# Output weights of a cached decode step: rows of 4 KB for four heads in place of 2 KB for two

## The chip, the cores and the metric

The kernel runs on one core of a Trainium2 chip. The metric is the device time of one launch in microseconds (us), as a median of several runs; runs of most kernels agree within about 0.3 us, apart from a few that are 1 to 2 us longer. A run of one core alone has its state settled by the other runs of the same kernel; all profiled runs used here count as fast. The profile comes from one execution, whose span is about 1.8 us shorter than its device time.

## The reference

Two attention blocks decode one token each for 4 batches and 32 heads of 128, and their outputs are concatenated. Block A has 8 key heads and a window of 2048 positions; block B, the full-cache part, has 32 key heads and all 8192 positions. B moves most of the bytes.

```python
def _B_ref(x, k_cache, v_cache, wq, wo):          # x 4x1x512, caches 4x32x8192x128, bf16
    q = (x @ wq).reshape(B, Sq, H, Dh).transpose(0, 2, 1, 3)
    scores = jnp.einsum("bhqd,bhkd->bhqk", q, k_cache) * (Dh ** -0.5)
    p = _softmax(scores, axis=-1)
    o = jnp.einsum("bhqk,bhkd->bhqd", p, v_cache)
    return o.transpose(0, 2, 1, 3).reshape(B, Sq, H * Dh) @ wo   # wo 4096x512
```

## The kernel before

B is cut into 64 chunks, each two heads of one batch: 4 MB of keys and 4 MB of values, double-buffered. TensorE transposes the keys in groups of 8 tiles into PSUM, VectorE and ScalarE copy ("evict") them to SBUF, TensorE forms the scores, and after the softmax multiplies the values with the probabilities. The outputs of two chunks (a *pair*) are multiplied with the output weights. In the program the 8 chunks of A come first, so c - NCA counts the chunks of B; TensorE's instructions for a pair are a loop body wherever two pairs have equal instructions and waits that grow evenly.

The output weights of two heads are loaded with two consecutive rows of `wo` on one partition, 2 KB per partition. The outputs must then be spread in the same order, row 2p+r to partition p, slot r. A small matmul with a 0/1 matrix (`sel2`) does it. A mask `pm` lets a pair's half of the batches through and zeroes the other.

```python
def dma_wos(hp):
    src = B_wo[2 * hp * P:2 * (hp + 1) * P, :].rearrange("(p r) n -> p (r n)", r=2)
    sch.add_dma("sp", lambda e: e.dma_start(wos[:, :, :].rearrange("p r n -> p (r n)"), src), "d_wos",
                waits=[("fin", NCA + 4 * hp - 1)] if hp else [], key=("wos", hp))
# ... in norm_out, full cache: rz holds 1 / sum times the mask pm
o, i0 = oz[:, :].rearrange("p (x y) -> p x y", x=2), bcast(po[:, 0:4], [[0, 2], [1, 4]])
i1 = rz[:, :].rearrange("p (x y) -> p x y", x=2)
# ... in emit_sel, full cache (k = 2, n = 8)
sel, x, n, z, k = sel2, oz[:, :], 8, zB[:, :], 2
for r in range(k):
    pe_mm(ms[:, Z0 + r * n:Z0 + (r + 1) * n], sel[:, r, :], x, ...)
for h in range(k):
    pp = slice(h * P // k, (h + 1) * P // k)
    src = ms[pp, Z0:Z0 + k * n].rearrange("p (r b h) -> p h r b", r=k, b=NB)[:, h]
    sch.add("dve", lambda e, src=src, pp=pp: e.tensor_copy(z[pp, :].rearrange("p (r b) -> p r b", r=k), src), ...)
# ... in emit_fin, full cache; each of ops in two halves of 256 columns, to partitions 0 and 64
ops = [(zB[:, r * NB:(r + 1) * NB], wos[:, r, :]) for r in range(2)]
# ...
def emit_wol():      # once, in the last chunk: the last two heads' weights in plain order
    for u in range(2):
        o = tr[:, u, :].bitcast(F32)
        for r in range(2):
            pe_mm(o, back2[:, u, r, :], wos[:, r, :], start=r == 0, stop=r == 1, ...)
```

`emit_wol`, the *re-layout*, serves the very end: the outputs of the last pair go straight into the last product, without selection, so their weights must lie in plain row order. It is issued between value tiles 64 and 65 of the last chunk, whose values arrive in five pieces.

Of the kernel before, what the change touches and what calls it, by code (L numbers as in the profile page):

```python
# [7 lines left out]
ALU = mybir.AluOpType  # L8
AX = mybir.AxisListType
BF16 = mybir.dt.bfloat16  # L10
F32 = mybir.dt.float32

P = 128
# [6 lines left out]
NSM = 2  # L20
# [139 lines left out]
def bass_concat_heads__sliding_block_cached__mha_block_cached__decode_kernel(  # L160
# [45 lines left out]
    with ExitStack() as es:  # L206
        block = es.enter_context(nc.Block())

        def sb(name, shape, dt):
            return es.enter_context(nc.sbuf_tensor(name, shape, dt))  # L210
# [6 lines left out]
        wos = sb("wos", [P, 2, DO], BF16)  # L217
# [19 lines left out]
        rz = sb("rz", [P, 8], F32)  # L237
        pm = sb("pm", [P, HB // 2 + 1, 2, 2, 4], F32)
        pbt = {0: sb("pba", [P, NPB, NTA * 16 + NW], BF16), 1: sb("pbb", [P, NPB, NTB * 2 + NW], BF16)}
        oT = sb("oT", [P, NSM, 16], BF16)  # L240
        oz = sb("oz", [P, 8], BF16)
# [3 lines left out]
        sel2 = sb("sel2", [P, 2, P], BF16)  # L245
        back2 = sb("back2", [P, 2, 2, P], BF16)
        zA = sb("zA", [P, 2, 16], BF16)
        zB = sb("zB", [P, 8], BF16)
# [29 lines left out]

        sch.add("pool", lambda e: e.memset(pm[:, :, :, :, :], 0.0), key="c_pm0")
        for x in range(2):  # L280
            sch.add("pool", lambda e, x=x: e.memset(pm[:, 1:, x, x, :], 1.0), waits=["c_pm0"], key="c_pm" if x else None)
# [9 lines left out]
        for r in range(2):  # L291
            sch.add("pool", lambda e, r=r: e.affine_select(
                out=sel2[:, r, :], in_=onesb[:, :], pattern=[[0, 2], [-2, 64]], compare_op=ALU.is_equal,
                fill=0.0, base=-r, channel_multiplier=1))
            for u in range(2):
                sch.add("pool", lambda e, r=r, u=u: e.affine_select(
                    out=back2[:, u, r, :], in_=onesb[:, :], pattern=[[1, P]], compare_op=ALU.is_equal,
                    fill=0.0, base=P * u - r, channel_multiplier=-2), key="c_sel" if r == u == 1 else None)
# [37 lines left out]
        def dma_wos(hp):  # L336


            src = B_wo[2 * hp * P:2 * (hp + 1) * P, :].rearrange("(p r) n -> p (r n)", r=2)
            sch.add_dma("sp", lambda e: e.dma_start(wos[:, :, :].rearrange("p r n -> p (r n)"), src), "d_wos",  # L340
                        waits=[("fin", NCA + 4 * hp - 1)] if hp else [], key=("wos", hp))
# [45 lines left out]
        for kind, c in loads:  # L387
            if kind == "k" and c >= NCA and (c == NCA or (c - NCA) % 4 == 3 and c > NCA + 3):
                dma_wos((c - NCA) // 4)
            dma_kv(kind, c)  # L390
            if kind == "v" and c > NCA and (c - NCA) % 2 == 1:


                hp = max(0, c - NCA - 2) // 4
                sch.add("sp", lambda e: e.sem_inc(sems["eng_sp"], 1), waits=[("wos", hp)] + (["kl"] if c == NC - 1 else []),
                        key=("wos2", c - 2 if c > NCA + 1 else NONE), self_inc=True)
            if kind == "v" and c < NCA:
                dma_wo(c)
        sch.add("sp", lambda e: e.sem_inc(sems["eng_sp"], 1), waits=[("wos", HB // 2 - 1)], key=("wos2", NC - 1), self_inc=True)
# [115 lines left out]
        def bcast(ap, dims):  # L515
            return bass.AP(ap.tensor, ap.offset, [ap.ap[0]] + dims)
# [122 lines left out]
        def norm_sum(c):  # L639
            if 0 <= c < NCA:  # L640
                m, n, rs, ri = c % NSM, 16, rst[0][:, c % NSM, :], rinv[:, c % NSM, :]
            else:
                m, n, rs, ri = NSM, 4, rst[1][:, :], rinv[:, 0, 0:4]
            pe_mm(ms[:, L0:L0 + n], onesf[:, :], rs, waits=([("rs", c), "c_onesf"] if c != NONE else []) + ms_read, key=("L", c))
            sch.add("dve", lambda e: e.reciprocal(out=ri, in_=ms[:, L0:L0 + n]), waits=[("L", c)], key=("rinv", c))
            if c >= NCA or c == NONE:

                pair = 4 * (c - NCA - 1 + 4) if c != NONE else 8
                pv = pm[:, :, :, :, :].rearrange("p a b c d -> p (a b c d)")
                sch.add("dve", lambda e, x=0: e.tensor_tensor(  # L650
                    out=rz[:, :].rearrange("p (x y) -> p x y", x=2), in0=bcast(ri, [[0, 2], [1, 4]]),
                    in1=pv[:, bass.ds(x + pair, 8)].rearrange("p (x y) -> p x y", x=2), op=ALU.mult),
                    waits=[("rinv", c), "c_pm"], key=("rz", c), at=pair)
            ms_read[:] = [("rinv", c)]
            rs_read[m] = [("L", c)]

        def norm_out(c):
            if 0 <= c < NCA:
                m = c % NSM
                o, i0, i1 = oT[:, m, :], po[:, m * 16:m * 16 + 16], rinv[:, m, :]  # L660
            else:

                o, i0 = oz[:, :].rearrange("p (x y) -> p x y", x=2), bcast(po[:, 0:4], [[0, 2], [1, 4]])
                i1 = rz[:, :].rearrange("p (x y) -> p x y", x=2)
            waits = [("rinv" if 0 <= c < NCA else "rz", c), ("pv", c)] + ([("sm", c - 2 if c != NCA + 1 else NONE)] if c >= 2 else [])
            sch.add("dve", lambda e: e.tensor_tensor(out=o, in0=i0, in1=i1, op=ALU.mult), waits=waits, key=("oT", c))  # L666
            po_read[:] = [("oT", c)]

        def emit_sel(c):

            if 0 <= c < NCA:
                sel, x, n, z, k = sel4, oT[:, c % NSM, :], 16, zA[:, c % 2, :], 4
                free = [("fin", c - 2)] if c >= 2 else []
            else:
                sel, x, n, z, k = sel2, oz[:, :], 8, zB[:, :], 2
                free = [("fin", c - 2 if c - 2 >= NCA else NONE)] if c != NONE else []
            for r in range(k):
                pe_mm(ms[:, Z0 + r * n:Z0 + (r + 1) * n], sel[:, r, :], x,
                      waits=[("oT", c)] + ms_read if r == 0 else [], key=("sm", c) if r == k - 1 else None)
            for h in range(k):  # L680
                pp = slice(h * P // k, (h + 1) * P // k)
                src = ms[pp, Z0:Z0 + k * n].rearrange("p (r b h) -> p h r b", r=k, b=NB)[:, h]
                sch.add("dve", lambda e, src=src, pp=pp: e.tensor_copy(z[pp, :].rearrange("p (r b) -> p r b", r=k), src),  # L683
                        waits=[("sm", c)] + free if h == 0 else [], key=("z", c) if h == k - 1 else None)
            ms_read[:] = [("z", c)]

        def emit_wol():

            for u in range(2):
                o = tr[:, u, :].bitcast(F32)  # L690
                for r in range(2):
                    pe_mm(o, back2[:, u, r, :], wos[:, r, :], start=r == 0, stop=r == 1,
                          waits=[("wos2", NC - 1)] if u == r == 0 else [], key=("back", u) if r else None)
# [5 lines left out]
        def emit_fin(c):  # L699
            ab = 0 if 0 <= c < NCA else 1  # L700
            if c == NC - 1:
                ov = oz[:, :].rearrange("p (b u) -> p b u", u=2)
                ops = [(ov[:, :, u], wol[:, u, :]) for u in range(2)]
                waits = [("oT", c), ("wol", 0), ("wol", 1)]
            elif ab == 1:
                ops = [(zB[:, r * NB:(r + 1) * NB], wos[:, r, :]) for r in range(2)]
# [174 lines left out]
```

## Time and profile before

| | |
|---|---|
| device time | 1374.14 us (1374.09 to 1374.22, 3 runs) |
| span of the profile | 1372.6 us |
| DMA queue of the loads | 99.8% of the time of 16 engines |
| TensorE, VectorE, ScalarE busy | 86%, 48%, 32% |
| TensorE waiting for keys, full cache | 141.5 us in 58 waits |
| output weights, full cache | 16 loads of 256 KB, 2048 packets of 2 KB |

The row that decides is the third: the loads fill the DMA engines from start to end. A busy share of 86% on TensorE is not a bound, since its waits for keys are part of the same profile. The prediction below shows the lines.

### The profile page before, as it was taken

To read this page: it belongs to the slowest core of one execution; us is meant where nothing else is said; L and a number is where in the kernel's file an instruction comes from. 1 tells how busy PE (TensorE), PEld (TensorE's weight loads), DVE (VectorE), ACT (ScalarE), POOL (GpSimd) and SP (SyncE) were. 2 spreads that over 40 slices of the span, in tenths; PEclk is the share of its full clock that TensorE was granted. 3 is DMA by queue.
4 is the path that set the end of the run, shared out by engine and by line. 5 is a ranking of instruction groups with operands and counts; after the bars stand their busy time and mean duration, and the time that the engine had idled before them with its cause. 6 is when DMAs were issued, how large, how long until landed. Compare 5 with 4: busy or idle time off the path is not lost.

```text
span 1372.6 us, 59967 instructions
## 1 busy us (share of the span) xinstructions
PE 1176.5 (86%) x27065; PEld 1132.9 (83%) x27067; DVE 656.6 (48%) x1434; ACT 434.7 (32%) x650; POOL 7.3 (1%) x28
## 2 busy tenths in 40 slices
PE   4888898889888888988888888888898888888888
PEld 4777898888888888888888878888898888888888
DVE  1775454445444444454445444444454444444544
ACT  1553232333223322332233323322333233323322
POOL 2000000000000000000000000000000000000000
PEclk9998999999999999999999999999999999999999
DMA  9999999999999999999999999999999999999998
GB/s 400 423 424 432 429 433 428 433 432 432 432 431 433 429 434 428 434 430 434 430 434 430 430 433 432 432 431 433 429 433 431 434 429 434 430 432 432 432 427 352
DMA packets 25261, 587.53 MB, mean 428 GB/s; under 512 B 2820, under 2 KB 2840, under 8 KB 6296
## 3 DMA queue, kind: packets, MB, share of 16 engines
q1 hardware_dynamic: 25208, 587.22, 99.8%
q8 instruction: 16, 0.26, 0.1%
q14 instruction: 5, 0.04, 0.0%
q10 hardware_dynamic: 32, 0.01, 0.0%
HBM read 587.21 MB, written 0.01 MB: 428 GB/s over the span
## 4 chain that ended last, share of the span: by engine, by line
DMA 65%; PE 33%; issue 1%; DVE 1%; ACT 0%; SPq 0%; DVEq 0%
DMA kv<-in_B_k_cache_dram 57%; PE tr L408 21%; PE sc L410 9%; DMA kv<-in_A_k_cache_dram 5%; DMA kv<-in_B_v_cache_dram 3%; PE po L410 2%; PE fin L410 1%; PE ms L410 0%; ACT kt L476 0%; DVE sA L527 0%; SPq L365 0%; ACT pba L597 0%; PE ms L408 0%; DVE zA L683 0%; DVE rm L536 0%
## 5 line engine op out<-in xcount | busy, mean ns | idle before, releaser
L408 PE MATMUL tr<-identb,kv 128*128 128x128 bf16 x8704 | 697.9, 230 | 148.8 <-DMA kv<-in_B_k_cache_dram 141.5
L478 DVE COPY kt<-tr 128x1024 bf16<-128x1024 bf16 x736 | 502.6, 690 | 457.1 <-PE tr L408 452.7
L408 PEld LDWEIGHTS tr<-identb,kv 128*128 128x128 bf16 x8704 | 552.9, 104 | 165.2 <-DMA kv<-in_B_k_cache_dram 81.7
L476 ACT ACTIVATE kt<-tr 128x1024 bf16<-128x1024 bf16 x352 | 359.3, 1023 | 666.8 <-PE tr L408 666.7
L410 PE MATMUL sc<-qb,kt 128*128 128x64 bf16 x8704 | 446.2, 196 | 14.3 <-ACT kt L476 12.8
L410 PEld LDWEIGHTS sc<-qb,kt 128*128 128x128 bf16 x8704 | 366.4, 100 | 26.0 <-ACT kt L476 20.2
L410 PE MATMUL po<-pbb,kv 128*128 128x64 bf16 x8320 | 284.4, 192 | 4.5 <-issue 3.9
L410 PEld LDWEIGHTS po<-pbb,kv 128*128 128x128 bf16 x8320 | 263.2, 97 | 7.1 <-issue 4.1
L577 ACT ACTIVATE pbb<-sc,negb 64x128 bf16<-64x128 f32 x128 | 51.6, 403 | 254.3 <-DVE negb L564 253.5
L541 DVE TENSOR_REDUCE rm<-sc 64x1 f32<-64x128 f32 x128 | 37.0, 289 | 56.6 <-PE sc L410 55.7
L553 DVE TENSOR_REDUCE gm<-ms 1x2 f32<-1x128 f32 (+1 forms) x72 | 20.1, 279 | 48.4 <-PE ms L408 48.4
L564 DVE COPY negb<-ms 128x1 f32<-128x1 f32 (+1 forms) x72 | 11.4, 158 | 47.0 <-PE ms L410 46.8
L410 PE MATMUL ms<-identf,gx 1*128 1x1 f32 (+1 forms) x144 | 27.2, 256 | 0.8 <-DVE zA L683 0.8
L666 DVE TENSOR_TENSOR oz<-po,rz 128x8 bf16<-128x8 f32 x33 | 5.5, 166 | 40.7 <-PE po L410 40.7
L410 PEld LDWEIGHTS ms<-identf,gx 1*128 1x128 f32 (+1 forms) x144 | 21.1, 182 | 4.6 <-DVE zA L683 0.9
L577 ACT ACTIVATION_READ_ACCUMULATOR pbb<-sc,negb 64x1 f32 x128 | 23.7, 185 | 0.0
L410 PE MATMUL po<-pba,kv 128*128 128x64 bf16 x512 | 20.5, 199 | 3.5 <-issue 2.1
L410 PEld LDWEIGHTS po<-pba,kv 128*128 128x128 bf16 x512 | 17.9, 102 | 5.7 <-ACT pba L597 4.2
L408 PE MATMUL ms<-identf,rm 128*1 128x128 f32 (+1 forms) x72 | 19.5, 271 | 2.4 <-DVE rm L536 2.3
L557 DVE TENSOR_SCALAR gx<-gm 1x128 f32<-1x128 f32 (+1 forms) x72 | 16.0, 222 | 2.5
L683 DVE CAST zB<-ms 64x8 bf16<-64x8 f32 x64 | 10.5, 164 | 9.2 <-PE ms L410 8.7
L410 PE MATMUL ms<-xT,kv 128*128 128x4 bf16 x256 | 7.1, 166 | 8.8 <-DMA kv<-in_A_wq_dram 5.0
(61 smaller groups left out, 173.9 us busy)
## 6 DMA issues: line engine op xcount, KB each, us to landing
kv<-in_B_k_cache_dram SPq DMA_DIRECT2D x63, 4096.0 KB, 26.5
kv<-in_B_v_cache_dram SPq DMA_DIRECT2D x63, 4096.0 KB, 30.9
kv<-in_A_k_cache_dram SPq DMA_DIRECT2D x8, 2048.0 KB, 14.8
kv<-in_A_v_cache_dram SPq DMA_DIRECT2D x8, 2048.0 KB, 16.2
kv<-in_A_wq_dram SPq DMA_DIRECT2D x1, 4096.0 KB, 12.5
kv<-in_B_wq_dram SPq DMA_DIRECT2D x1, 4096.0 KB, 27.1
wor<-in_A_wo_dram SPq DMA_DIRECT2D x8, 512.0 KB, 9.8
wos<-in_B_wo_dram SPq DMA_DIRECT2D x16, 256.0 KB, 20.3
```

Source lines behind the costliest of these rows:

```text
L408: sch.add("pe", lambda e: e.transpose(o, l, r), waits, key)
L410: sch.add("pe", lambda e: e.matmul(o, l, r, start=start, stop=stop), waits, key)
L476: sch.add("act", lambda e: e.activation(dst, src, ACTF.Copy), waits=waits, key=("ev", s))
L478: sch.add("dve", lambda e: e.tensor_copy(dst, src), waits=waits, key=("ev", s))
L541: sch.add("dve", lambda e, src=src, pp=pp: e.tensor_reduce(out=rm[pp, m, 0:1], in_=src, axis=AX.X, op=ALU.max), waits=[("S", ch["s_last"]) ...
L553: sch.add("dve", lambda e: e.tensor_reduce(out=gm[0:C, m, 0:U], in_=src, axis=AX.X, op=ALU.max), waits=[("trm", c)], key=("gmax", c))
L557: sch.add("dve", lambda e: e.tensor_scalar(out=dst, in0=gv, scalar1=-scale, scalar2=None, op0=ALU.mult), waits=[("gmax", c)], key=("gx", c))
L564: sch.add("dve", lambda e: e.tensor_copy(negb[:, m, 0:C], ms[:, col:col + C]), waits=[("bc", c)], key=("negb", c))
L577: sch.add("act", lambda e, src=src, pp=pp, n=n, u=u: e.activation(probs_of(c)[pp, :, u], src, ACTF.Exp, bias=negb[pp, m, 0:1], scale=scale ...
L666: sch.add("dve", lambda e: e.tensor_tensor(out=o, in0=i0, in1=i1, op=ALU.mult), waits=waits, key=("oT", c))
L683: sch.add("dve", lambda e, src=src, pp=pp: e.tensor_copy(z[pp, :].rearrange("p (r b) -> p r b", r=k), src), waits=[("sm", c)] + free if h ...
```

## The change

The intent is fewer and longer packets: weights of four heads with four rows, 4 KB, on a partition, in half as many loads. The price is on the compute engines: outputs are spread over four places per pair (two pairs of heads by two halves of the batches), three of them zeroed by the mask, so selection and output products double, and the re-layout takes eight matmuls for four. The diff, cut to its core:

```diff
-        wos = sb("wos", [P, 2, DO], BF16)
+        wos = sb("wos", [P, 4, DO], BF16)
...
-        pm = sb("pm", [P, HB // 2 + 1, 2, 2, 4], F32)
+        pm = sb("pm", [P, HB + 2, 2, 2, 4], F32)
...
-            src = B_wo[2 * hp * P:2 * (hp + 1) * P, :].rearrange("(p r) n -> p (r n)", r=2)
+            src = B_wo[4 * hq * P:4 * (hq + 1) * P, :].rearrange("(p r) n -> p (r n)", r=4)
...
-                        waits=[("fin", NCA + 4 * hp - 1)] if hp else [], key=("wos", hp))
+                        waits=[("fin", NCA + 8 * hq - 1)] if hq else [], key=("wos", hq))
...
-                o, i0 = oz[:, :].rearrange("p (x y) -> p x y", x=2), bcast(po[:, 0:4], [[0, 2], [1, 4]])
+                o, i0 = oz[:, :].rearrange("p (x y) -> p x y", x=4), bcast(po[:, 0:4], [[0, 4], [1, 4]])
...
-                sel, x, n, z, k = sel2, oz[:, :], 8, zB[:, :], 2
+                x, z, order = oz[:, :], zB[:, :], "p (r s b u) -> p s u r b"
...
-                for r in range(2):
-                    pe_mm(o, back2[:, u, r, :], wos[:, r, :], start=r == 0, stop=r == 1,
+                for r in range(4):
+                    pe_mm(o, back4[:, u, r, :], wos[:, r, :], start=r == 0, stop=r == 3,
...
-                ops = [(zB[:, r * NB:(r + 1) * NB], wos[:, r, :]) for r in range(2)]
+                ops = [(zB[:, r * NB:(r + 1) * NB], wos[:, r, :]) for r in range(4)]
```

More of the change, by code (lines that the diff above doesn't have):

```diff
@@ L236, in bass_concat_heads__sliding_block_cached__mha_block_cached__decode_kernel @@
         rinv = sb("rinv", [P, NSM, 16], F32)
-        rz = sb("rz", [P, 8], F32)
-        pm = sb("pm", [P, HB // 2 + 1, 2, 2, 4], F32)
+        rz = sb("rz", [P, 16], F32)
+        pm = sb("pm", [P, HB + 2, 2, 2, 4], F32)
         pbt = {0: sb("pba", [P, NPB, NTA * 16 + NW], BF16), 1: sb("pbb", [P, NPB, NTB * 2 + NW], BF16)}
         oT = sb("oT", [P, NSM, 16], BF16)
-        oz = sb("oz", [P, 8], BF16)
+        oz = sb("oz", [P, 16], BF16)
         outsb = sb("outsb", [36, DO], BF16)
@@ L244, in bass_concat_heads__sliding_block_cached__mha_block_cached__decode_kernel @@
         sel4 = sb("sel4", [P, 4, P], BF16)
-        sel2 = sb("sel2", [P, 2, P], BF16)
-        back2 = sb("back2", [P, 2, 2, P], BF16)
+        back4 = sb("back4", [P, 2, 4, P], BF16)
         zA = sb("zA", [P, 2, 16], BF16)
-        zB = sb("zB", [P, 8], BF16)
+        zB = sb("zB", [P, 16], BF16)
         wol = sb("wol", [P, 2, DO], BF16)
@@ L279, in bass_concat_heads__sliding_block_cached__mha_block_cached__decode_kernel @@
         sch.add("pool", lambda e: e.memset(pm[:, :, :, :, :], 0.0), key="c_pm0")
-        for x in range(2):
-            sch.add("pool", lambda e, x=x: e.memset(pm[:, 1:, x, x, :], 1.0), waits=["c_pm0"], key="c_pm" if x else None)
+        for i in range(4):
+            sch.add("pool", lambda e, i=i: e.memset(pm[:, 2 + i::4, i // 2, i % 2, :], 1.0), waits=["c_pm0"], key="c_pm" if i == 3 else None)
         sch.add("pool", lambda e: e.memset(pbt[0][:, :, :], 0.0), key=("c_pb", 0))
@@ L290, in bass_concat_heads__sliding_block_cached__mha_block_cached__decode_kernel @@
                 fill=0.0, base=-r, channel_multiplier=1), waits=["c_onesb"])
-        for r in range(2):
-            sch.add("pool", lambda e, r=r: e.affine_select(
-                out=sel2[:, r, :], in_=onesb[:, :], pattern=[[0, 2], [-2, 64]], compare_op=ALU.is_equal,
-                fill=0.0, base=-r, channel_multiplier=1))
+        for r in range(4):
             for u in range(2):
                 sch.add("pool", lambda e, r=r, u=u: e.affine_select(
-                    out=back2[:, u, r, :], in_=onesb[:, :], pattern=[[1, P]], compare_op=ALU.is_equal,
-                    fill=0.0, base=P * u - r, channel_multiplier=-2), key="c_sel" if r == u == 1 else None)
+                    out=back4[:, u, r, :], in_=onesb[:, :], pattern=[[1, P]], compare_op=ALU.is_equal,
+                    fill=0.0, base=2 * P + P * u - r, channel_multiplier=-4), key="c_sel" if r == 3 and u == 1 else None)
         half_of = {}
@@ L334, in dma_wo, with dma_wos @@
                         waits=[("fin", g - 2)] if g >= 2 and slot < 2 else [], key=("wo", g))
-        def dma_wos(hp):
-            src = B_wo[2 * hp * P:2 * (hp + 1) * P, :].rearrange("(p r) n -> p (r n)", r=2)
+        def dma_wos(hq):
+            src = B_wo[4 * hq * P:4 * (hq + 1) * P, :].rearrange("(p r) n -> p (r n)", r=4)
             sch.add_dma("sp", lambda e: e.dma_start(wos[:, :, :].rearrange("p r n -> p (r n)"), src), "d_wos",
-                        waits=[("fin", NCA + 4 * hp - 1)] if hp else [], key=("wos", hp))
+                        waits=[("fin", NCA + 8 * hq - 1)] if hq else [], key=("wos", hq))
         def dma_kv(kind, c):
@@ L387, in bass_concat_heads__sliding_block_cached__mha_block_cached__decode_kernel @@
         for kind, c in loads:
-            if kind == "k" and c >= NCA and (c == NCA or (c - NCA) % 4 == 3 and c > NCA + 3):
-                dma_wos((c - NCA) // 4)
+            if kind == "k" and c >= NCA and (c == NCA or (c - NCA) % 8 == 3 and c > NCA + 3):
+                dma_wos((c - NCA) // 8)
             dma_kv(kind, c)
             if kind == "v" and c > NCA and (c - NCA) % 2 == 1:
-                hp = max(0, c - NCA - 2) // 4
-                sch.add("sp", lambda e: e.sem_inc(sems["eng_sp"], 1), waits=[("wos", hp)] + (["kl"] if c == NC - 1 else []),
+                hq = max(0, c - NCA - 2) // 8
+                sch.add("sp", lambda e: e.sem_inc(sems["eng_sp"], 1), waits=[("wos", hq)] + (["kl"] if c == NC - 1 else []),
                         key=("wos2", c - 2 if c > NCA + 1 else NONE), self_inc=True)
@@ L398, in bass_concat_heads__sliding_block_cached__mha_block_cached__decode_kernel @@
                 dma_wo(c)
-        sch.add("sp", lambda e: e.sem_inc(sems["eng_sp"], 1), waits=[("wos", HB // 2 - 1)], key=("wos2", NC - 1), self_inc=True)
+        sch.add("sp", lambda e: e.sem_inc(sems["eng_sp"], 1), waits=[("wos", HB // 4 - 1)], key=("wos2", NC - 1), self_inc=True)
         ms_read = []
@@ L646, in norm_sum @@
             if c >= NCA or c == NONE:
-                pair = 4 * (c - NCA - 1 + 4) if c != NONE else 8
+                pair = 16 * ((c - NCA - 1) // 2 + 2) if c != NONE else 16
                 pv = pm[:, :, :, :, :].rearrange("p a b c d -> p (a b c d)")
                 sch.add("dve", lambda e, x=0: e.tensor_tensor(
-                    out=rz[:, :].rearrange("p (x y) -> p x y", x=2), in0=bcast(ri, [[0, 2], [1, 4]]),
-                    in1=pv[:, bass.ds(x + pair, 8)].rearrange("p (x y) -> p x y", x=2), op=ALU.mult),
+                    out=rz[:, :].rearrange("p (x y) -> p x y", x=4), in0=bcast(ri, [[0, 4], [1, 4]]),
+                    in1=pv[:, bass.ds(x + pair, 16)].rearrange("p (x y) -> p x y", x=4), op=ALU.mult),
                     waits=[("rinv", c), "c_pm"], key=("rz", c), at=pair)
@@ L661, in norm_out @@
             else:
-                o, i0 = oz[:, :].rearrange("p (x y) -> p x y", x=2), bcast(po[:, 0:4], [[0, 2], [1, 4]])
-                i1 = rz[:, :].rearrange("p (x y) -> p x y", x=2)
+                o, i0 = oz[:, :].rearrange("p (x y) -> p x y", x=4), bcast(po[:, 0:4], [[0, 4], [1, 4]])
+                i1 = rz[:, :].rearrange("p (x y) -> p x y", x=4)
             waits = [("rinv" if 0 <= c < NCA else "rz", c), ("pv", c)] + ([("sm", c - 2 if c != NCA + 1 else NONE)] if c >= 2 else [])
@@ L671, in emit_sel @@
             if 0 <= c < NCA:
-                sel, x, n, z, k = sel4, oT[:, c % NSM, :], 16, zA[:, c % 2, :], 4
+                x, z, order = oT[:, c % NSM, :], zA[:, c % 2, :], "p (r b h) -> p h r b"
                 free = [("fin", c - 2)] if c >= 2 else []
             else:
-                sel, x, n, z, k = sel2, oz[:, :], 8, zB[:, :], 2
+                x, z, order = oz[:, :], zB[:, :], "p (r s b u) -> p s u r b"
                 free = [("fin", c - 2 if c - 2 >= NCA else NONE)] if c != NONE else []
-            for r in range(k):
-                pe_mm(ms[:, Z0 + r * n:Z0 + (r + 1) * n], sel[:, r, :], x,
-                      waits=[("oT", c)] + ms_read if r == 0 else [], key=("sm", c) if r == k - 1 else None)
-            for h in range(k):
-                pp = slice(h * P // k, (h + 1) * P // k)
-                src = ms[pp, Z0:Z0 + k * n].rearrange("p (r b h) -> p h r b", r=k, b=NB)[:, h]
-                sch.add("dve", lambda e, src=src, pp=pp: e.tensor_copy(z[pp, :].rearrange("p (r b) -> p r b", r=k), src),
-                        waits=[("sm", c)] + free if h == 0 else [], key=("z", c) if h == k - 1 else None)
+            for r in range(4):
+                pe_mm(ms[:, Z0 + r * 16:Z0 + (r + 1) * 16], sel4[:, r, :], x,
+                      waits=[("oT", c)] + ms_read if r == 0 else [], key=("sm", c) if r == 3 else None)
+            for h in range(4):
+                pp = slice(h * P // 4, (h + 1) * P // 4)
+                if 0 <= c < NCA:
+                    src = ms[pp, Z0:Z0 + 64].rearrange(order, r=4, b=NB)[:, h]
+                else:
+                    src = ms[pp, Z0:Z0 + 64].rearrange(order, r=4, s=2, b=NB)[:, h // 2, h % 2]
+                sch.add("dve", lambda e, src=src, pp=pp: e.tensor_copy(z[pp, :].rearrange("p (r b) -> p r b", r=4), src),
+                        waits=[("sm", c)] + free if h == 0 else [], key=("z", c) if h == 3 else None)
             ms_read[:] = [("z", c)]
@@ L690, in emit_wol @@
                 o = tr[:, u, :].bitcast(F32)
-                for r in range(2):
-                    pe_mm(o, back2[:, u, r, :], wos[:, r, :], start=r == 0, stop=r == 1,
-                          waits=[("wos2", NC - 1)] if u == r == 0 else [], key=("back", u) if r else None)
+                for r in range(4):
+                    pe_mm(o, back4[:, u, r, :], wos[:, r, :], start=r == 0, stop=r == 3,
+                          waits=[("wos2", NC - 1)] if u == r == 0 else [], key=("back", u) if r == 3 else None)
                 if u == 0:
@@ L701, in emit_fin @@
             if c == NC - 1:
-                ov = oz[:, :].rearrange("p (b u) -> p b u", u=2)
+                ov = oz[:, 8:16].rearrange("p (b u) -> p b u", u=2)
                 ops = [(ov[:, :, u], wol[:, u, :]) for u in range(2)]
```

## The prediction

> **What bounds the kernel now.** I read the page's DMA lines first, because the reference is one decode step that reads every cached key and value once, and then the chain that ended last.
>
> ```profile
> DMA  9999999999999999999999999999999999999998
> DMA packets 25261, 587.53 MB, mean 428 GB/s; under 512 B 2820, under 2 KB 2840, under 8 KB 6296
> ...
> q1 hardware_dynamic: 25208, 587.22, 99.8%
> ...
> DMA 65%; PE 33%; issue 1%; DVE 1%; ACT 0%; SPq 0%; DVEq 0%
> DMA kv<-in_B_k_cache_dram 57%; PE tr L408 21%; PE sc L410 9%; DMA kv<-in_A_k_cache_dram 5%; DMA kv<-in_B_v_cache_dram 3%; PE po L410 2%; PE fin L410 1%; PE ms L410 0%; ACT kt L476 0%; DVE sA L527 0%; SPq L365 0%; ACT pba L597 0%; PE ms L408 0%; DVE zA L683 0%; DVE rm L536 0%
> ```
>
> The 16 DMA engines are busy in every one of the 40 slices, and one queue fills 99.8% of their time. TensorE in the chain is no contradiction: a key load is issued when the transposes of the chunk two before it have freed its buffer, so the chain alternates between transposes and loads. But that load lands a median 26.5 us after its issue (page, part 6), while its 4 MB need about 9.7 us at 431 GB/s (the rate over 278 to 1328 us in the view by stretches). So some 16 us of other loads stand ahead of it, and a late issue of a microsecond or two costs nothing. TensorE itself waits for data:
>
> ```profile
> PE tr L408 <- DMA kv<-in_B_k_cache_dram: 141.5, 58, 4.1
> ```
>
> That is 141.5 / 58 = 2.4 us in each of 58 chunks of the 64, or some 4.9 us in each pair of chunks. In the full-cache part, work added on TensorE, VectorE or ScalarE is therefore free up to that, and bytes, or time per byte, on the DMA engines are not. The end is another regime. Its timeline, from the last value matmuls (columns: start, duration, engine, line, operation, operands, count, idle before it):
>
> ```profile
> 1364.10 2.05 PE L410 MATMUL po<-pbb,kv 128*128 128x64 bf16 x64
> ...
> 1366.20 0.81 PE L410 MATMUL tr<-wos,back 128*128 128x512 bf16 x3
> ...
> 1366.85 2.03 PE L410 MATMUL po<-pbb,kv 128*128 128x64 bf16 x56
> ...
> 1369.10 0.29 PEld L410 LDWEIGHTS po<-pbb,kv 128*128 128x128 bf16 x8 [0.35 <-DMA kv<-in_B_v_cache_dram]
> 1369.11 0.41 PE L410 MATMUL po<-pbb,kv 128*128 128x64 bf16 x8 [0.23 <-DMA kv<-in_B_v_cache_dram]
> 1369.62 0.17 DVE L666 TENSOR_TENSOR oz<-po,rz 128x8 bf16<-128x8 f32 x1 [1.88 <-PE po L410]
> 1369.84 0.38 PE L410 MATMUL fin<-wol,oz 128*4 128x256 bf16 x4 [0.33 <-DVE oz L666]
> ```
>
> Here TensorE is nearly full, and the last piece of V beats it by only 0.23 to 0.35 us of waiting. The re-layout of the last output weights (the matmuls into tr from wos and back) stands in front of the last 64 value matmuls. A change to either side of this near-tie shows in the end time.
>
> **What the Trainium skill says.** "Perfetto Trace Analysis", section Roofline, calls about 435 GB/s, the 16 DMA engines together, the practical ceiling of a single core; the trace agrees with 431 GB/s in the long middle stretch. "DMA: Bandwidth & Descriptors", section Why small descriptors are slow (HBM only), says that each packet costs a small fixed time beside its bytes. The trace has it: in its record of every DMA packet the mean is 84.6 ns at 2 KB (2304 packets), 161.4 ns at 4 KB (1152) and 1218 ns at 32 KB (16384). From the first two, 2 KB more costs 76.7 ns, so the fixed part is 84.6 - 76.7 = 7.9 ns. The same page's Specifications ask for 512 B and more for line rate; rows of 2 KB are already past that, so little is left to win. "TensorE: Matmul & The Clock Gate", section Back-to-back issue gap, gives about 216 ns between isolated matmuls of 512 columns; the three recorded in the tail give (0.81 - 0.379) / 2 = 0.216 us, with 0.379 us the duration of one, so the trace agrees (the fourth's record is missing).
>
> **The change part by part.**
>
> *Loads of output weights.* Now 16 loads of 256 KB, in rows of 2 KB; then 8 of 512 KB in rows of 4 KB. Bytes are unchanged, 4.2 MB of 587. 2048 packets x 84.6 ns / 16 engines = 10.83 us become 1024 x 161.4 / 16 = 10.33 us. Eight loads fewer also drop 8 x 16 four-byte completion packets of 9.1 ns, 0.07 us per engine. Gain on the DMA engines: 0.57 us. As they are full throughout, the last V piece should land 0.57 us earlier.
>
> *Selection of rows, per pair of chunks (32 pairs).* Two matmuls of 8 columns become four of 16: the sliding-window part already does just that, four in 0.24 us against two in 0.20 us, so +0.04 us on TensorE. Two copies to zB of 164 ns become four of half the partitions and twice the columns: +0.33 us on VectorE, 10.5 us in all. VectorE is 48% busy and idles 452.7 us for transposes, so this hides, bar perhaps 0.2 us of delay for one key eviction.
>
> *Output matmuls per pair.* Four of 256 columns become eight. They go in twos to partitions 0 and 64 and overlap: four took 0.38 us where one takes 0.272, so each further two cost 0.107 us. Eight take 0.59 us: +0.21 us.
>
> Together TensorE gains 0.25 us per pair, 8 us over the run. It takes a twentieth of the 4.9 us of waiting per pair: nothing of it on the path until the last pair.
>
> *Masks and spread.* rz and oz have 16 columns for 8. At 166 ns both are at their fixed cost (the reciprocal over 4 columns takes 172): about +10 ns each, one of them on the final path.
>
> *Set-up on GpSimd.* Two selects more of 0.29 us, a larger mask memset and two more small ones: about +1.1 us, from an end at 8.3 us to about 9.4. TensorE needs the selects only after the second query product, after 32 us: hidden.
>
> *The tail.* The re-layout needs eight matmuls of 512 columns for four: 4 x 0.216 = +0.86 us on TensorE between value tiles 64 and 65 of the last chunk. Before that point TensorE resumes at 1359.2 us after waiting 0.46 to 0.58 us for the values of the last chunk but one. That wait shrinks: the values come 0.57 us sooner, the extra selection and output matmuls of the last pair make TensorE up to 0.25 us later, so it starts 0.1 to 0.4 us sooner. The loads of weights for the 56 value tiles end at 1368.76; with -0.1 to -0.4 and +0.86 that is 1369.2 to 1369.5, less up to 0.2 us of waiting for pieces of V inside the 56 (56 matmuls in 2.03 us where the 64 before ran at 29.5 ns a step, 1.8 us for 56). So the last eight start at 1369.0 to 1369.5 against 1369.10 now: between 0.1 us sooner and 0.4 later, with the data by then there (landing at 1369.06 - 0.57 = 1368.5).
>
> The sum: the DMA gain of 0.57 us is real, but TensorE takes the tail over and gives it back. Net about +0.15 us: 1374.3 us.
>
> **The rivals.**
>
> *The whole DMA gain arrives.* If TensorE in the tail has more slack than I read (the re-layout overlapping the value matmuls), the end moves by -0.57 us, to 1373.6. For it: the chain's last long piece is a load, V from 1329.92 for 39.14 us. Against it: only 0.35 us of idle time between the 56 and the last eight.
>
> *The whole tail cost arrives.* If the values do not come sooner, +0.86 minus 0.35 of wait is +0.5, and eviction delays of the last selection add 0.2: 1374.9.
>
> *Small descriptors cost more than their packets show.* If each issue makes the queue run dry for a moment, eight issues fewer win more. SyncE spends 0.33 us on issuing one and waits in front of it:
>
> ```profile
> SPq L340 <- PE fin L410: 165.7, 15, 13.3
> ```
>
> Those 165.7 us look tempting, half of them gone with half the loads. But the key load behind it could not go much sooner: it waits for its own transposes too (3.3 us later in the one I followed, 1241.88 and then 1245.15). With 99.8% of engine time filled, dry time cannot exceed 0.2% of the span, 2.7 us, most of which is the start and the end. Best case some -1.5 us: 1372.6.
>
> *A new wait.* A 512 KB load lands 0.6 us later than one of 256 KB, and SyncE waits for it before later loads. That delays a key issue with 16 us of loads ahead of it: nothing.
>
> *TensorE or VectorE becomes the bound.* It would need 4.9 us more per pair; the change adds 0.25 and 0.35.
>
> **Range and chances.** All terms lie between -1.5 and +0.8 us, and the three runs of before lie within 0.13 us. The centre is 1374.3, range 1373.5 to 1375.2. Two per cent is 27 us, which no term approaches; 2% in all for something not seen, split evenly.
>
> **What would show it.** Right: 2048 packets of 2 KB replaced by 1024 of 4 KB, the last V piece landing about 0.6 us sooner (near 1368.5), no idle time for V in front of the last eight value matmuls, and about 0.86 us more between the two runs of value matmuls; waits of transposes for keys near 134 us, 8 us less. Wrong: a wait of transposes on VectorE or on SyncE's weights in the middle, DMA slices under 9, or last V landing no sooner. The prediction would be off by more than its range only if the queue runs dry somewhere.

## The result

| | before | changed |
|---|---|---|
| median of the series | 1374.22 us (1374.09 to 1374.29, 5 runs) | 1373.64 us (1373.51 to 1373.89, 5 runs) |
| span of the profile | 1372.6 us | 1371.8 us |
| output-weight packets, full cache | 2048 of 2 KB | 1024 of 4 KB |
| sum of all packet times / 16 engines | 1370.60 us | 1369.63 us |
| TensorE waiting for keys | 141.5 us | 135.9 us |

The ratio is 0.9996 (95% interval 0.9981 to 1.0011): the same at the 2% level. A ratio is the mean time of one kernel's fast runs over that of the other's of the same rounds, so not quite the ratio of the medians. The difference of 0.58 us is small, but no run of one kernel overlaps with a run of the other. The result lies in the predicted range, on the other side of the old time from its centre. The two profiles are of executions of 1374.43 and 1373.59 us, 0.84 us apart, so they show more of a gain than the medians.

The page of the changed kernel, parts 2 to 4 (DMA share in 40 slices, packets, the loads' queue, and the chain by engine):

```profile
DMA  9999999999999999999999999999999999999998
DMA packets 24108, 587.52 MB, mean 428 GB/s; under 512 B 2692, under 2 KB 2712, under 8 KB 5144
...
q1 hardware_dynamic: 24056, 587.22, 99.7%
...
DMA 60%; PE 38%; issue 1%; DVE 1%; ACT 0%; SPq 0%; DVEq 0%
```

There are 1152 packets fewer in this queue (25208 before): 1024 from the longer rows and 128 completion packets of the eight loads that are gone. Bytes and the full queue are as before. TensorE's share of the chain has grown from 33% to 38%. Some 0.8 points of this come from the tail (about 11 us), where the chain now runs on TensorE; the rest is not explained. That such a share is not the share of work on the path is tested in runs 9 and 10. The view of waits of the changed kernel (engine and line that waits, what it waits for, total us, times, longest):

```profile
PE tr L405 <- DMA kv<-in_B_k_cache_dram: 135.9, 58, 4.7
...
SPq L337 <- PE fin L407: 89.1, 7, 13.5
```

TensorE still waits for keys in the middle, 5.6 us less in sum here. With the repeats it is 140.3 and 141.5 us before and 135.9 to 138.4 after; that the added matmuls went into these waits fits, and runs 9 and 10 test it. SyncE's wait in front of the weight loads fell from 165.7 to 89.1 us with half the loads. Those 77 us were not on the path: run 2 has as short a wait (81.7 us) and the time of the kernel before.

The tail decides the rest. First the wait for the values of the last chunk but one, in the timeline of the kernel before and then of the changed one:

```profile
1359.21 0.64 PE L410 MATMUL po<-pbb,kv 128*128 128x64 bf16 x16 [0.46 <-DMA kv<-in_B_v_cache_dram]
```

```profile
1358.27 0.65 PE L407 MATMUL po<-pbb,kv 128*128 128x64 bf16 x16 [0.21 <-DMA kv<-in_B_v_cache_dram]
...
1363.16 2.04 PE L407 MATMUL po<-pbb,kv 128*128 128x64 bf16 x64
...
1365.01 1.42 PEld L407 LDWEIGHTS tr<-wos,back 128*128 128x128 bf16 x8
1365.26 1.67 PE L407 MATMUL tr<-wos,back 128*128 128x512 bf16 x7
...
1366.77 2.04 PE L407 MATMUL po<-pbb,kv 128*128 128x64 bf16 x64
...
1368.91 0.17 DVE L663 TENSOR_TENSOR oz<-po,rz 128x16 bf16<-128x16 f32 x1 [1.25 <-PE po L407]
```

The values come 0.94 us sooner (1358.27 against 1359.21). From there the changed kernel runs TensorE without a wait to the end: the 56 and 8 value matmuls of before have merged into one run of 64 with no idle time in front of the last eight. From the start of those values to the last normalisation (oz) it takes 1368.91 - 1358.27 = 10.64 us; before, 1369.62 - 1359.21 = 10.41. So in these two profiles the loads gain 0.94 us, the longer tail on TensorE gives back 0.23, and 0.71 us remain at this point, against 0.84 between the times of these two executions and 0.58 between the medians.

Part of the 0.94 is the luck of these profiles. Run 1's profile of the changed kernel agrees (1358.25, of an execution of 1373.57 us), but run 12's, of the slowest execution of its series (1373.96 us), has

```profile
1358.57 0.64 PE L407 MATMUL po<-pbb,kv 128*128 128x64 bf16 x16
```

which is 0.64 us sooner than before and without a wait for V in front, and its oz stands at 1369.19, only 0.43 us sooner. The tail is as long there (10.62 us).

Where in the run the gain arises is seen by asking, in the packet records of the loads' queue, at which time a given number of bytes has been moved (each packet's bytes spread evenly over its time). The changed kernel is behind by 0.06 us at 80 MB and ahead by 0.17 at 200, 0.38 at 400 and 0.68 at 580 MB, and still by 0.68 at 586. It is a slow gain, as a saving in packets should give. The rest of the 0.94 lies in the spread of the 16 engines, since a load has landed when its slowest engine is done: the first piece of the last V landed from 1360.35 to 1364.05 us before and from 1359.75 to 1363.11 after. This spread was between 2.9 and 3.8 us in the six traces with the loads of the changed kernel and a looped last pair, so the smaller one is not shown to be an effect of the change. The last piece of V landed at 1368.13 us against 1369.06.

### The profile page after: what moved, and what is told of

Its sections match the earlier page's. It is cut to its first block, busy times and chain, and to the rows that moved or that the text cites. A ratio compares the mean times of both kernels' runs of the same rounds, so it can differ in the third digit from the quotient of the medians.

```text
span 1371.8 us, 60419 instructions
## 1 busy us (share of the span) xinstructions
PE 1181.6 (86%) x27261; PEld 1137.0 (83%) x27263; DVE 665.2 (48%) x1498; ACT 434.7 (32%) x650; POOL 8.1 (1%) x32
## 4 chain that ended last, share of the span: by engine, by line
DMA 60%; PE 38%; issue 1%; DVE 1%; ACT 0%; SPq 0%; DVEq 0%
DMA kv<-in_B_k_cache_dram 55%; PE tr L405 23%; PE sc L407 9%; PE po L407 3%; DMA kv<-in_B_v_cache_dram 2%; DMA kv<-in_B_wq_dram 2%; PE fin L407 2%; DMA kv<-in_A_k_cache_dram 1%; PE ms L407 1%; ACT kt L473 0%; DVE sA L524 0%; DVE rm L533 0%; PE ms L405 0%; PE tr L407 0%; DVE sA L522 0%
## 5 line engine op out<-in xcount | busy, mean ns | idle before, releaser
L405 PE MATMUL tr<-identb,kv 128*128 128x128 bf16 x8704 | 695.6, 230 | 140.9 <-DMA kv<-in_B_k_cache_dram 135.9
L683 DVE CAST zB<-ms 32x16 bf16<-32x16 f32 x128 | 21.8, 170 | 11.1 <-PE ms L407 9.8
L663 DVE TENSOR_TENSOR oz<-po,rz 128x16 bf16<-128x16 f32 x33 | 5.8, 174 | 40.5 <-PE po L407 40.5
L407 PE MATMUL fin<-wos,zB 128*4 128x256 bf16 x256 | 19.3, 272 | 0.0
```

The lines of the kernel that those rows point to most:

```text
L405: sch.add("pe", lambda e: e.transpose(o, l, r), waits, key)
L407: sch.add("pe", lambda e: e.matmul(o, l, r, start=start, stop=stop), waits, key)
L663: sch.add("dve", lambda e: e.tensor_tensor(out=o, in0=i0, in1=i1, op=ALU.mult), waits=waits, key=("oT", c))
```

## The experiments

There were twelve kernels in three series. All were correct. Each series ran on another chip (15, 4, 12), with the kernel before beside it: medians 1374.19, 1374.14 and 1374.22 us.

**1. The changed kernel once more** (no edit).

> The changed kernel unaltered, for the spread of its time and of its packet durations. My theory: its 0.58 us gain over the kernel before is real and stays: 1373.3 to 1373.9 us, with a 4 KB packet at 161 ns and the last piece of V landed some 0.6 to 0.9 us sooner than before. Rival, a lucky series: anywhere from 1373.5 to 1374.4, overlapping the runs of the kernel before.

Measured: 1373.83 us (1373.57 to 1373.87, 5 runs) beside 1374.19 (1374.04 to 1374.39) of before. Its values of the last chunk but one start at 1358.25 us, its packets add up to 1369.69 us per engine. The gain holds, here as 0.36 us. All later numbers of the first series are set against this run.

**2. The loads split again, computation kept.**

```diff
-            sch.add_dma("sp", lambda e: e.dma_start(wos[:, :, :].rearrange("p r n -> p (r n)"), src), "d_wos", ...)
+            for h in range(2):
+                x = slice(2 * h * DO, 2 * (h + 1) * DO)     # 2 KB of each partition
+                sch.add_dma("sp", lambda e, x=x: e.dma_start(dst[:, x], src[:, x]), "d_wos", ...)
```

> Changed kernel, but each load of output weights split into two of 256 KB with rows of 2 KB: the transfer half of the change undone, its computation kept. My theory (2048 packets of 84.6 ns for 1024 of 161.4, and 128 completion packets of 9 ns, on 16 full DMA engines): 0.57 us more than the changed kernel, 1374.2 us, and since TensorE starts its tail when the values of the last chunk but one land, all of it shows. Rival, the gain has nothing to do with packets (fewer waits of SyncE on the output matmuls, which stay at 7 here): 1373.6. Rival, the tail's extra re-layout shows in full once the loads are late: 1374.5 or more.

Measured: 1374.33 us (1374.21 to 1374.54, and one of 1375.63). That is 0.50 us above the changed kernel and 0.14 above the kernel before. The timeline of this run:

```profile
1358.96 0.64 PE L410 MATMUL po<-pbb,kv 128*128 128x64 bf16 x16 [0.18 <-DMA kv<-in_B_v_cache_dram]
```

The values start at 1358.96, 0.71 us after those of the changed kernel, with SyncE's waits on the output matmuls still 7. So the gain is in the transfers, rows and issues together, and not in SyncE's waits or in the order of the loads, which are those of the changed kernel. The computation of the change with the old rows gives about the time of the kernel before (0.14 us more, within the spread). Packets add up to 1370.46 us per engine, 0.77 more than in run 1, and 0.50 of it arrived in the time.

**3. The same eight loads in rows of 512 B.** The destination gets a gap of 32 B after each 512 B, which breaks the rows up.

```diff
-        wos = sb("wos", [P, 4, DO], BF16)
+        wos = sb("wos", [P, 4, 2, DO // 2 + 16], BF16)
...
-            e.dma_start(wos[:, :, :].rearrange("p r n -> p (r n)"), src)
+            e.dma_start(wos[:, :, :, 0:DO // 2].rearrange("p r h n -> p (r h) n"), src)
```

> Changed kernel, 8 loads as before it, but in rows of 512 B: 8192 packets for 1024, the same bytes, issues and waits. My theory (7.9 ns fixed plus 19.2 ns of bytes = 27.1 ns each; 13.9 us per engine for 10.3): 3.5 us more than the changed kernel, 1377.2 us. Rival, small packets hide behind others in the same engine or the loads are not what bounds: below 1374.5. Rival, 512 B rows cost more than the fixed part fitted at 2 and 4 KB: above 1379.

Measured: 1377.39 us (1377.32 to 1378.37), 3.56 us above the changed kernel. The page shows the packets:

```profile
DMA packets 31276, 587.52 MB, mean 427 GB/s; under 512 B 2692, under 2 KB 10904, under 8 KB 12312
```

Under 2 KB there are 8192 more than in the changed kernel. A packet of 512 B took 29.5 ns in the mean, more than the 27.1 expected. The same bytes, issues and waits cost 3.6 us more because of packets alone: these loads are on the path. That 3.5 was hit is in part luck, since two errors cancel. At 29.5 ns the weights' own packets cost 4.8 us more, and all packets together 5.5 (1375.20 us per engine), of which about two thirds arrived, as in run 2.

**4. The re-layout before the last chunk but one.** This was meant as a better version: TensorE waits there for keys anyway.

```diff
+            if c == NC - 2:
+                emit_wol()                 # into banks 1 and 2 of tr; the transposes wait for its copies
             for g in range(ch["NG"]):
...
-            if g == LASTV[0] // TG - 1:
-                emit_wol()
```

> Changed kernel, but the re-layout of the last output weights (eight matmuls of 512 columns) is done before the transposes of the last chunk but one, where TensorE waits some 2 us for keys, not between the value matmuls of the last chunk. My theory (TensorE takes the tail over from the loads, by about 0.35 us): 0.3 to 0.4 us less than the changed kernel, 1373.3 us, and a wait for the last piece of V comes back in front of the last eight value matmuls. Rival, the loads still bound the tail of the changed kernel: no change, 1373.6. Rival, TensorE alone bounds it and the pieces of V are long there: 1.7 us less, 1371.9.

Measured: 1377.25 us (1376.88 to 1377.74), 3.4 us *slower* than the changed kernel. None of the theories had this. The timeline of TensorE has gaps that no semaphore explains ("issue"):

```profile
1346.00 0.63 PE L407 MATMUL po<-pbb,kv 128*128 128x64 bf16 x16 [1.68 <-issue]
...
1352.47 0.27 PE L405 MATMUL tr<-identb,kv 128*128 128x128 bf16 x2 [0.93 <-issue]
...
1358.77 0.35 PE L407 MATMUL sc<-qb,kt 128*128 128x64 bf16 x6 [0.46 <-issue]
...
1364.96 1.08 PE L407 MATMUL po<-pbb,kv 128*128 128x64 bf16 x31 [1.19 <-issue]
...
1370.06 2.38 PE L407 MATMUL po<-pbb,kv 128*128 128x64 bf16 x76 [0.57 <-issue]
```

They come every 6 us. The page counts 22 instruction packets in q8, 0.36 MB, for 16 and 0.26 MB in the changed kernel, and the packet records put six of 16 KB at 1337 to 1368 us, 5 to 7 us apart. Each of the five gaps ends 2.3 to 2.5 us after the start of one of them. The last pair now differs from the others, so it had left TensorE's loop and its instructions had to be fetched in line. That is tested in run 8.

**5. The kernel before once more** (no edit).

> The kernel before unaltered. My theory (the changed kernel's gain is real): 1374.0 to 1374.4 us, no overlap with the changed kernel's 1373.5 to 1373.9, and 2 KB packets at 84 to 85 ns again. Rival, a drift between series: a median below 1374.0.

Measured: 1374.31 us (1374.09 to 1374.34). Its packets add up to 1370.68 us, its values start at 1359.23 us. The difference between the two kernels is not a drift.

**6. The re-layout done twice.**

```diff
-                for r in range(4):
+                for k in range(8):
+                    r = k % 4              # start at r == 0 clears, so the result is the same
```

> Changed kernel with the eight matmuls of the re-layout in the last chunk done twice. My theory (TensorE, not the loads, bounds the tail of the changed kernel, with no slack left in front of the last eight value matmuls): all of 8 x 0.216 = 1.73 us shows, 1375.4 us. Rival, the last pieces of V bound it: with about 0.4 us between their landing and the last matmuls hidden either way, at most 1.3 us shows, below 1375.0; if the re-layout is hidden altogether 1373.7.

Measured: 1375.33 us (1375.18 to 1375.67), 1.5 to 1.7 us above the three series of the changed kernel (1373.64, 1373.83, 1373.67). The timeline:

```profile
1365.36 3.15 PEld L407 LDWEIGHTS tr<-wos,back 128*128 128x128 bf16 x16
1365.60 3.40 PE L407 MATMUL tr<-wos,back 128*128 128x512 bf16 x15
...
1368.84 2.03 PE L407 MATMUL po<-pbb,kv 128*128 128x64 bf16 x64
```

Nearly all of the added work (1.73 us) shows. After the change, TensorE bounds the tail.

**7. The re-layout in row groups.** For each head only 32 of the 128 rows of the mask are not zero.

```diff
-                    pe_mm(o, back4[:, u, r, :], wos[:, r, :], ...)
+                    pp = slice(P // 2 + u * P // 4, P // 2 + (u + 1) * P // 4)     # 64 to 95, 96 to 127
+                    pe_mm(o[u], back4[pp, u, r, :], wos[pp, r, :], ...)            # u alternates
```

> Changed kernel, but each matmul of the re-layout contracts only the 32 rows that its selection mask does not zero, and the two heads (row groups 64 to 95 and 96 to 127) alternate, so that they may overlap. My theory: with overlap the re-layout takes 0.87 instead of 1.73 us; the last eight value matmuls then wait for the last piece of V, and only 0.3 to 0.4 us of the 0.86 shows: 1373.35 us. Rival, row groups do not overlap here: 1373.7, and the re-layout still 1.7 us long.

Measured: 1373.56 us (1373.24 to 1373.72). The timeline:

```profile
1365.06 1.03 PE L407 MATMUL tr<-wos,back 32*128 32x512 bf16 x8
1366.02 1.70 PEld L407 LDWEIGHTS po<-pbb,kv 128*128 128x128 bf16 x56 [0.42 <-DMA kv<-in_B_v_cache_dram]
1366.03 1.82 PE L407 MATMUL po<-pbb,kv 128*128 128x64 bf16 x56
...
1368.05 0.29 PEld L407 LDWEIGHTS po<-pbb,kv 128*128 128x128 bf16 x8 [0.33 <-DMA kv<-in_B_v_cache_dram]
```

The eight matmuls now take 1.03 us. The groups overlap, and the wait for V is back in front of the last eight: TensorE's 0.86 us have become waiting. In this trace, of the fastest execution of its five (1373.24 us), oz stands at 1368.57, 0.34 us sooner than in the changed kernel, but the median is within the noise of the changed kernel; run 11 repeats it.

**8. Only the loop broken.** The re-layout stays in its place; one wait that has long been met is added in the last pair.

```diff
+                    waits += ["c_sel"] if c == NC - 2 and g == 1 else []
```

> Changed kernel with the re-layout in its place, but one wait that is long over (on the masks' set-up) added in the last pair of chunks, which takes that pair out of TensorE's loop as the early re-layout did. My theory of the failed early re-layout (the unlooped instructions, some 1000 more, are fetched in blocks of 16 KB while the loads fill the DMA engines, and TensorE stands still at each block): 1377 to 1379 us, 22 instruction packets of 16 KB for 16, and gaps of 0.5 to 1.7 us on TensorE some 6 us apart with no semaphore behind them. Rival, the early re-layout itself (its banks and waits) cost the time: 1373.7.

Measured: 1378.49 us (1378.40 to 1378.63, and one of 1380.21), 4.7 to 4.9 us above the three series of the changed kernel. The page and the timeline:

```profile
q8 instruction: 22, 0.36, 0.1%
```

```profile
1363.56 0.83 PE L407 MATMUL po<-pbb,kv 128*128 128x64 bf16 x23 [1.25 <-issue]
...
1369.76 0.27 PE L407 MATMUL po<-pbb,kv 128*128 128x64 bf16 x3 [1.66 <-issue]
```

A wait that waits for nothing costs almost 5 us, because it takes one pair out of the loop. The four gaps without a semaphore (1.41, 0.48, 1.25 and 1.66 us) add up to 4.80 us, all of the added time, and each ends 2.4 to 2.6 us after the start of a 16 KB instruction packet. So run 4 failed by the loop. Between the two unlooped kernels, the early re-layout is 1378.49 - 1377.25 = 1.24 us faster, in line with a TensorE-bound tail.

**9 and 10. Idle matmuls in the middle**, 20 and 60 per pair:

```diff
+                if NCA <= c < NC - 2 and c % 2 == 0 and g == 3:
+                    for _ in range(20):                                   # 60 in the other
+                        pe_mm(po[:, 256:512], identb[:, :], sel4[:, 0:2, :])
```

> Changed kernel with 20 idle matmuls of 256 columns (into unused columns of po) in every pair of full-cache chunks but the last: about 20 x 0.11 = 2.2 us of TensorE per pair, 68 us in all, ten times what the change adds there. My theory (TensorE waits 4.7 us for keys in each pair, and two loads of 4 MB stand in the queue ahead of a late issue): no change, 1373.3 to 1374.2 us, and the waits of transposes for keys fall from 136 to about 68 us. Rival, the 38% of the chain that TensorE holds is work on the path: up to 68 us more, 1442 us.

> The same with 60 idle matmuls per pair, 6.6 us. My theory: the 4.7 us of waiting per pair is used up and the rest, 1.9 us x 31 pairs = 59 us, shows: 1420 to 1440 us, with almost no wait for keys left and DMA slices below 9. Rival, the slack is larger than the waits show (below 1400) or there is none (1373.7 + 205 = 1578 us).

Measured: 1379.51 us (1379.08 to 1380.47) and 1386.65 us (1385.19 to 1387.72), 5.8 and 13.0 us above the changed kernel of the same series, for 76.6 and 208.1 us of added matmuls (busy time on the pages). "No change" was wrong for the first, and 59 us was wrong for the second. Part of it is my edit: sparing the last pair again took it out of the loop (22 and 23 instruction packets). To keep that apart, compare only the middle. The view by stretches, 240 to 1300 us (length; busy us and instructions of TensorE, weight loads, VectorE, ScalarE, GpSimd; granted clock, DMA share, GB/s), of the changed kernel and then of the one with 60:

```profile
240.00:1300.00 1060.00, 919.55 (x21327) 892.39 (x21325) 507.31 (x1110) 326.31 (x487) 0.00 (x0) 0.94 1.00 432
```

```profile
240.00:1300.00 1060.00, 1046.57 (x23119) 1002.10 (x23116) 507.60 (x1117) 327.89 (x492) 0.00 (x0) 1.00 1.00 431
```

TensorE works 127 us more in the same stretch and the DMA engines move the same GB/s. From 100 to 580 MB moved, the changed kernel takes 1112.2 us, that with 20 idle matmuls 1112.3, that with 60 idle matmuls 1113.0. The middle is free, then, even of 6.6 us per pair. Nearly all the added time arises at the ends: with 20 and 60, the loads fall behind by 1.1 and 8.1 us before 100 MB (slices of the second page drop to 389 and 384 GB/s; why the first pairs lose so much is not shown), and the rest comes at the unlooped last pair, whose gaps without a semaphore add up to 4.6 and 4.1 us. The waits show where the room came from:

```profile
PE tr L405 <- DMA kv<-in_B_k_cache_dram: 4.7, 4, 1.3
```

The waits for keys have gone from 135.9 to 4.7 us, but the added work was 208 us. The other part is the clock. After a long wait TensorE ran slowly for a while: in the changed kernel the first 24 transposes of a chunk took 1.62 to 2.74 us after all 29 waits of 1.8 us and more, and 1.51 us or less in 32 of the other 34 chunks. With idle matmuls in place of waits the granted clock (as a share of full speed) in the middle rose from 0.94 to 1.00 and the mean transpose fell from 231 to 219 ns. Waiting time understates the room.

**11 and 12. Row groups and the changed kernel in one series.**

> The re-layout in row groups again, in one series with the changed kernel, to see whether its 0.1 to 0.3 us holds. My theory (0.32 us in the trace, the tail then waiting for V): 1373.2 to 1373.6 us, below the changed kernel of this series. Rival, noise: equal medians.

> The changed kernel in the same series as the row groups: 1373.5 to 1373.9 us, below every run of the kernel before.

Measured: 1373.70 us (1373.49 to 1373.73) and 1373.67 us (1373.63 to 1373.96), beside 1374.22 (1373.96 to 1374.34) of before. One run of the changed kernel equals the lowest of the kernel before, so "below every run" just failed; the medians are 0.55 us apart. The row groups do not beat the changed kernel in this series, so the expectation failed. Their trace again has the short re-layout and the wait for V. The two medians together with run 7 leave a gain of 0 to 0.1 us, which is not told from nothing. No version tried clearly beats the changed kernel.

## Why the prediction was right or wrong

The prediction was right in its range and in its class, and wrong in the sign of its centre: +0.15 us was forecast, -0.36 to -0.58 was measured in three series. Point by point:

*The bound is the loads, and bytes or time per byte count in full.* Right as to the bound, not as to "in full". Run 3 changed the rows alone, run 2 rows and number of issues, and the time followed: +3.56 us for 3.5 worked out, +0.50 for 0.57. But by the packets as measured, only about two thirds arrived (3.56 of 5.5 us and 0.50 of 0.77). Why is open.

*"Gain on the DMA engines: 0.57 us."* This term was somewhat too small. By the bytes moved the loads are 0.68 us ahead at 580 MB (0.70 in run 1, 0.46 in run 12), and the packets add up to 0.97 us less per engine. The named parts were right: packets of 2 and 4 KB together gained 0.47 us, completion packets 0.07. These and the next term make 0.84 of the 0.97 us; some 0.1 is not assigned. The largest omission was the neighbours. The 32 KB packets of keys and values that started within 3 us of a weight load took 1220.7 ns in the mean in the kernel before (1844 packets, 15 loads) against 1217.1 elsewhere between 240 and 1340 us; in the changed kernel 1218.9 against 1216.9 (855 packets, 7 loads). That is 1844 x 3.6 / 16 = 0.41 us against 855 x 2.0 / 16 = 0.11: another 0.30 us. Both repeats (runs 1 and 5) have it. But it does not follow the row size alone. Run 2, with 2 KB rows in the seven places of the changed kernel, has 1220.5 ns against 1217.0 (894 packets), 0.20 us: two thirds of the 0.30 go with the number of places. In return its 2 KB packets themselves took longer, 86.2 ns for 84.6, which is 0.22 us. Near the 512 B rows of run 3 the neighbours took 1232.7 ns. That weight loads slow their neighbours is thus seen in the records; what this is worth of the time is not, as no run isolated it.

*Work in the middle is hidden.* Right, and by a wider margin than "a twentieth of the 4.9 us": run 10 hid 6.6 us per pair. Its 2.4 us of waiting per chunk is a mean: in the kernel before, TensorE stood idle for up to 1.85 us in front of 33 chunks and for 2.1 to 4.1 in front of 30. Zeroing, selection and output products came as worked out: the copies to zB grew from 10.5 to 21.8 us on VectorE, rz and oz by 8 to 9 ns each. Output products and selection grew by 7.0 and 1.7 us on TensorE, for 8 in all forecast; its whole busy time rose by 5.1 us, a sum that differs by 3 us between repeats. GpSimd's busy time grew by 0.8 us (1.1 forecast), and no new wait for it appears.

*"It starts 0.1 to 0.4 us sooner"* (the tail on TensorE). This is the step that failed. It started 0.94 us sooner here and in run 1, and 0.64 in run 12. The 0.25 us of extra work in the last pair was subtracted from the gain, but in the first two profiles TensorE was still waiting for these values after the change (0.21 us of the 0.46 left), so that work was hidden there as well, and the full gain of the loads counted. In run 12 the wait was gone: V landed at 1358.47 and TensorE came 0.1 us later. So the wait is nearly used up, and how often some of the extra work is paid, three profiles cannot tell.

*"+0.86 us on TensorE between value tiles 64 and 65"* and the slack against it. Right: from the first weight load of the re-layout to the next of the values it took 0.68 us before (1365.96 to 1366.64) and 1.54 after. What was hidden of it was close too: 0.63 us by the totals (0.86 - 0.23), where the prediction had up to 0.35 + 0.2. Run 6 shows that TensorE took the tail over: a second re-layout appears nearly in full (1.5 to 1.7 us of 1.73). Run 7 shows that the tie is still near: without 0.86 us of the re-layout, the last V stands in the way again.

*The rivals.* "The whole DMA gain arrives", -0.57 us to 1373.6, hit the number by another way: a larger gain less a tail cost, which is luck. "The whole tail cost arrives" is refuted by the 10.64 against 10.41 us. That fewer waits of SyncE keep the queue from running dry is refuted by run 2, which has the 7 waits of the changed kernel and the time of the kernel before. Whether an issue by itself costs something is not parted from the rows there, as run 2 has 16 issues; run 3, with 8, shows that rows alone cost time.

## What to carry to other kernels

Where the DMA engines are full, count packets and not only bytes: a packet had a fixed part of 7.9 ns here, worked out from rows of 2 and 4 KB (some 10 at 512 B), and large packets next to small ones took longer. Summed packet times overstated what arrived: two thirds did in runs 2 and 3. A profile shows one execution: repeat it before reading tenths of a microsecond from it. When the last transfers and an engine are nearly tied at the end, ask which wait stands first in that tail; work in front of a wait that remains is still free, work behind the last wait is paid. And before moving work to a "free" place in a looped program, ask whether it breaks the loop: one needless wait in the last pair cost almost 5 us here.

## What the Trainium skill lacked or had wrong

- "Runtime: NRT & Kernel Launch", section Instruction fetch mechanics, says that instructions are fetched in blocks of 16 KiB, that crossing a boundary is mostly hidden, and that kernels prefer full unrolling where possible. The blocks are seen here (16 KB packets). While the loads fill the DMA engines they are not hidden: run 8, with six blocks more, has gaps of 0.48 to 1.66 us on TensorE, 4.80 us in sum, and takes 4.7 to 4.9 us longer than the looped kernel.
- "DMA: Bandwidth & Descriptors", section Why small descriptors are slow (HBM only), gives a fixed overhead per packet in cycles. No page tells that small packets slow large ones beside them: packets of 32 KB took 1220.7 ns next to 2 KB rows and 1232.7 next to 512 B rows, for about 1217 elsewhere.
- "TensorE: Matmul & The Clock Gate", section Back-to-back issue gap, gives 131 ns per matmul of 512 columns in a real stream of weight load and matmul, and says that 216 over-counts. The sixteen such pairs of run 6 at full granted clock took (3.40 - 0.379) / 14 = 0.216 us each (15 recorded, 0.379 us the length of one).
- The same page's Part 1: The HAM clock gate (the "warmup" mystery) says that activity releases a throttled clock, which run 10 agrees with (granted clock 0.94 to 1.00 in the middle). It lacks the consequence for reading waits: the 208 us of matmuls added there found room although the waits for keys came to 135.9 us.
